# Block tables built in four parts, one branch at the end, output row numbers computed earlier

## The chip, the cores and the metric

The kernel runs on one core of one Trainium2 chip. The time is that of one whole launch, in device microseconds; of a kernel the median of several runs is given. Inputs and outputs lie in the chip's memory, and every step of the computation is in the launch.

## The reference

Three stages follow each other, in float32:

```
attention: state = alpha_t * state + k_t v_t^T ;  y_t = q_t state     (4 batches, 8 heads, 768 steps, 48 wide)
x = y as (3072 tokens, 384)
MoE 1, dense:  h = max(x @ w_in, 0);  x = (h * h) @ w_out              (384 -> 2048 -> 384)
MoE 2, top 1:  logits = x @ w_gate (8 experts);  e = argmax;  gate = softmax(logits)[e]
               eom = sigmoid(x @ w_output_gate)
               out[token] = gate * eom[e] * (max(x @ w1[e], 0) @ w2[e])  (384 -> 1024 -> 384)
```

Which expert a token goes to, and so how many tokens an expert has, is known only in the run.

## The kernel before

Tokens are handled in 24 tiles of 128, three tiles to a group (`GT`, 8 groups `NG`). Matrices that need float32's accuracy are split into two float16 halves (high and low) and multiplied in three passes; a row of a tile is scaled by a power of two that comes from its largest magnitude (`normalize`: `mxx`, `ebx`, `invx`, then the halves of `xr`, which DMA transposes to `xT`).

The first part of the program, up to about 551 us, is not written in its order. Each step (`add`) has a due time (`nominal(g, n)`: group g, n 28ths into it), an engine, a cost and the steps it depends on; `Plan.emit` simulates the engines and takes on each free engine the ready step with the smallest due time. Steps with two possible engines go to the second when the first is too far behind. A step is emitted whole: what it issues on an engine stands there in one piece. To this part belong the attention (`attend`), MoE 1 (`moe1_in`: h = x times w_in, `moe1_out`: o), the normalised rows of its result (`x2_out`: `row`), the routing of groups 0 to 6, and the splitting of w1 and w2 into halves (`split`: the load `spw`, the halves `spo`, a check `spj`, the store).

The second part is a loop written by hand over blocks of 128 tokens of one expert: b from 0 to 27 and one turn more to finish. A turn computes `s1(b, 0)` and `s1(b, 1)`, each eight 128-wide pieces' half of h: matmuls `hb`, then `part` (ScalarE copies, VectorE adds, twice per half), `rb` on ScalarE, and the two halves `hh` on VectorE. Beside it stand `s2(b - 1, ...)` (matmuls `ob`, ScalarE's `ot`, and a GpSimd DMA that writes 128 rows to their places in the output, by the row numbers `oi`), the gather of a later block's tokens by GpSimd (`gather`), and the transposes of the next block's tokens on TensorE (`turn_block`: `rt_ps`, copied by ScalarE to `xtb`).

Which tokens and which expert a block has stands in a table, computed by `table` in two pieces, from the counts of tokens per expert (a matmul, `pc`). The early table (groups 0 to 5 routed; 7 blocks, `NBA`) is one step of the planned part, `first_table`, due at `nominal(6, 14)`. The late table (the other 24 blocks) is a generator that the block loop advances: in the turn of block 2 its first part and its second part, in the turn of block 3 all that is left, before the gather of block 7. The loop stops at 28 blocks (`NBS`); if the counts need more (`more_i`), a first branch at the end runs blocks 28 to 30, and if a check of value ranges failed (`flag_i`), a second one runs a general version of everything. With these inputs neither is taken.

The functions that the change touches follow, with their line numbers.

Of the kernel before, what the change touches and what calls it, by code (L numbers as in the profile page):

```python
# [19 lines left out]
P = 128  # L20
NB, NH, NS, HD = 4, 8, 768, 48
NT = NB * NS
DM = 384
# [168 lines left out]
def moe_chain_kernel(ctx, tc, qka, vv, wi, wo, wg, w1, w2, out):  # L192
# [850 lines left out]
    def table(last):  # L1043
# [30 lines left out]
        lim = rt.tile([P, NE], F32, name="lim")  # L1074
        V.scalar_tensor_tensor(out=lim, in0=cnt, scalar=-1.0, in1=eoff, op0=ALU.add, op1=ALU.add)
        bb = rt.tile([P, NBB], F32, name="bb")[:, 0:nb]
        hi_ = rt.tile([P, 1], I32, name="hi_")
# [7 lines left out]
        if last:  # L1085
            V.tensor_scalar(out=more_i, in0=tot, scalar1=float(NBS - NBA), scalar2=None,
                            op0=ALU.is_gt)
        yield
        R = [P, nb, NE]
# [7 lines left out]
        if not last:  # L1097
# [14 lines left out]
            op=ALU.mult)  # L1112
        V.tensor_reduce(out=st, in_=big3, axis=AX.X, op=ALU.add)
        V.tensor_tensor(
            out=ohb, in0=ohb, in1=lim.rearrange("p (a e) -> p a e", a=1).to_broadcast(R),
# [108 lines left out]

    flag_i = const.tile([P, 1], I32, name="flag_i")

    def raise_flag():
# [43 lines left out]
    def raise_flag2(a):  # L1271
        V.tensor_reduce(out=a[:, 4:5], in_=rsum, axis=AX.X, op=ALU.max)
        V.scalar_tensor_tensor(out=a[:, 5:6], in0=a[:, 4:5], scalar=60000.0, in1=a[:, 0:1],
                               op0=ALU.is_le, op1=ALU.mult)
        pf = ps_r.tile([P, 1], F32, name="pf", tag="r")
        T.matmul(pf, onesf, a[:, 5:6], start=True, stop=True)
        V.tensor_scalar(out=flag_i, in0=pf, scalar1=float(P), scalar2=None, op0=ALU.is_lt)

# [37 lines left out]

    def load_w(b, k):
        if b >= lim[0]:
            return
        if k == 0:  # L1320
            wreg[b] = (nc.sync.value_load(e_i[0:1, b:b + 1], min_val=0, max_val=NE - 1),
                       nc.sync.value_load(ld_i[0:1, b:b + 1], min_val=0, max_val=1))
        e, ld = wreg[b]
        src = (w1s, w2s)[k]
        with tc.If(ld > 0):
            nc.sync.dma_start(
                out=wslot[b % NSLOT][k].rearrange(("p a c m -> p (a c) m",
                                                   "p a (c j) m -> p (a c) (j m)")[k],
                                                  **({}, {"j": 2})[k]),
                in_=src[bass.ds(e, 1)].rearrange(("e a c p m -> p (e a c) m",  # L1330
                                                  "e a c p j m -> p (e a c) (j m)")[k]))

    def s1(b, half):
# [4 lines left out]
        if half == 0:  # L1338
            c["hh"] = late[2].tile([P, 2, NFE, P], F16, name="hh", bufs=3)
        hh = c["hh"]  # L1340
        r = late[2].tile([P, 4, P], F32, name="rb")
# [22 lines left out]
    def s2(b, half):  # L1364
# [13 lines left out]
        if half == 1:  # L1378
            ot = late[2].tile([P, DM], F32, name="ot", bufs=2)
            row = c["row"]  # L1380
            S.activation(out=ot, in_=o, func=AF.Copy, scale=row[:, DM:DM + 1].bitcast(F32))  # L1381
            oi = late[2].tile([P, 1], I32, name="oi", bufs=3)
            V.tensor_tensor(out=oi, in0=row[:, DM + 1:], in1=pad_i[:, b:b + 1],
                            op=ALU.add)
            G.indirect_dma_start(  # L1385
# [4 lines left out]
    def switch_to_splits():  # L1390
        cvs.close()
        sp_pool[0] = sps.enter_context(tc.tile_pool(name="sp", bufs=2))

    def switch_to_blocks():
        sps.close()
        early.close()
        late[0] = lateS.enter_context(tc.tile_pool(name="late", bufs=2))
        for s in range(NSLOT):
            wslot[s] = (late[0].tile([P, 2, ND, EF], F16, name=f"w1_{s}", bufs=1),
                        late[0].tile([P, 2, NFE, DM], F16, name=f"w2_{s}", bufs=1))  # L1400

# [4 lines left out]
    def first_table():  # L1406
        r = ring("r_ps", 1)
        return add(nominal(NG - 2, 14), "V", 6643, lambda: list(table(False)), [route_done[NG - 3]],
                   new=[r])

    with tc.manual_schedule():
# [47 lines left out]
        for b in range(NBS + 1):  # L1459
# [11 lines left out]
            if b == 3:  # L1471
                for _ in tabling:
                    pass
                gather(b + 4)
            s1(b, 1)
            if b == 0:
                turn_last(1)
# [13 lines left out]
            s2(b - 1, 0)  # L1491
            if b == 2:
                tabling = table(True)
                next(tabling)
            if b >= 3:
                gather(b + 5)
# [6 lines left out]
            s2(b - 1, 1)  # L1503
            if b == 2:
                next(tabling)
            for n in loaded:
                exponent_check(n)
            if b >= 1:
                load_w(b - 1 + NSLOT, 1)
        more = nc.values_load(more_i[0:1, 0:1], min_val=0, max_val=1)  # L1510
        with tc.If(more > 0):
            lim[0] = NBLK
            for b in range(NBS, NBLK):
                load_w(b, 0)
                load_w(b, 1)
                gather(b)
                transp(b)
                for h in range(2):
                    s1(b, h)
                for h in range(2):  # L1520
                    s2(b, h)
            raise_flag2(fa)
        lateS.close()
# [174 lines left out]

    flag = nc.values_load(flag_i[0:1, 0:1], min_val=0, max_val=1)
    with tc.If(flag > 0):  # L1700
        fallback()

# [44 lines left out]
```

## Time and profile before

| | us |
|---|---|
| runs, median (lowest to highest) | 808.29 (807.83 to 808.43) |
| the profiled execution | 805.57 |
| its span in the profile | 803.8 |
| mean granted clock of TensorE | 0.969 of full speed |
| TensorE busy | 752.1 (94%) |
| VectorE busy | 588.5 (73%) |
| ScalarE busy | 506.5 (63%) |
| GpSimd busy | 347.1 (43%) |

TensorE is busy nearly throughout, so a microsecond is to be won where it waits or runs at its lower clock. The shares are means over stages with different limits; the sections below go by single stretches. PE is TensorE, DVE VectorE, ACT ScalarE, POOL GpSimd, SP SyncE (it issues most DMAs); a q behind the name is an engine's sequencer. L1048 is a line of the kernel.

### The profile page before, as it was taken

How to read it: one execution, taken by the hardware profiler on the slowest of the kernel's cores; microseconds unless marked ns; L12 is line 12 of the kernel's file. 1: busy time of each engine (PE TensorE's matmuls, PEld its weight loads, DVE VectorE, ACT ScalarE, POOL GpSimd, SP SyncE). 2: the span in 40 equal slices, each digit the busy share in tenths (PEclk: the TensorE clock that was granted, in tenths of full speed). 3: DMA queues.
4: the chain of work that ended last, by engine and by line, in shares of the span. 5: the costliest groups of instructions: out<-in, count | busy, mean ns of one | idle time of the engine just before them, and what ended most of it. 6: DMA issues, size and time to landing. Idle time of an engine off the chain costs nothing.

```text
span 803.8 us, 16848 instructions
## 1 busy us (share of the span) xinstructions
PE 752.1 (94%) x6066; PEld 514.9 (64%) x6066; DVE 588.5 (73%) x1370; ACT 506.5 (63%) x1167; POOL 347.1 (43%) x359
## 2 busy tenths in 40 slices
PE   8987789899997999999999997999989999999992
PEld 5755446665664666666666664657767777777871
DVE  7989969787887999999998886324745555555460
ACT  3378767676786888788887785644345555555540
POOL 4377736543464365586765551540132222232100
PEclk9999789999999999999999999999999999999996
DMA  9446661789949857969949747782739799892720
GB/s 265 112 134 173 180 184 50 207 236 295 313 125 280 239 145 197 275 169 239 259 121 300 191 120 227 190 311 83 263 96 348 250 355 356 272 387 94 246 74 21
DMA packets 156130, 168.48 MB, mean 210 GB/s; under 512 B 55340, under 2 KB 125004, under 8 KB 156032
## 3 DMA queue, kind: packets, MB, share of 16 engines
q1 hardware_dynamic: 150912, 152.25, 64.0%
q0 software_dynamic: 5120, 15.00, 5.6%
q8 instruction: 51, 0.84, 0.5%
q14 instruction: 47, 0.39, 0.1%
HBM read 120.52 MB, written 35.43 MB: 194 GB/s over the span
## 4 chain that ended last, share of the span: by engine, by line
PE 66%; DVE 15%; DMA 9%; issue 5%; ACT 2%; POOL 1%; SPq 0%; POOLq 0%; DVEq 0%; ACTq 0%
PE h L775 17%; PE o L814 15%; PE ob L1375 11%; PE hb L1352 8%; PE hb L1353 4%; DMA xT<-xr 3%; PE sp L597 2%; DMA x2T<-row 2%; DVE w L376 2%; PE idle L337 2%; DVE tb L370 2%; PE y L623 1%; DVE ta L364 1%; DMA a<-in_qka 1%; DMA spw<-in_w 1%
## 5 line engine op out<-in xcount | busy, mean ns | idle before, releaser
L775 PE MATMUL h<-xT,wi 128*128 128x384 f16 x1152 | 206.8, 333 | 24.3 <-DMA xT<-xr 14.8
L814 PE MATMUL o<-wo,g 128*128 128x385 f16 x1152 | 204.8, 331 | 2.3 <-POOL wo L391 1.4
L775 PEld LDWEIGHTS <-wi 128*128 128x128 f16 x1152 | 111.2, 99 | 102.2 <-issue 15.7
L312 POOL TENSOR_TENSOR g<-gg,g 128x384 f16<-128x384 f32 x115 | 125.3, 1098 | 90.0 <-ACT gg L793 58.8
L814 PEld LDWEIGHTS <-g 128*128 128x128 f16 x1152 | 111.0, 99 | 80.5 <-issue 7.2
L1352 PE MATMUL hb<-xtb,w 128*128 128x256 f16 x672 | 115.9, 275 | 3.8 <-ACT xtb L1306 3.7
L1375 PE MATMUL ob<-w,hh 128*128 128x384 f16 x672 | 117.8, 326 | 0.0
L1353 PE MATMUL hb<-xtb,w 128*128 128x128 f16 x672 | 114.1, 220 | 0.0
L1385 POOL DMA_INDIRECT out<-ot,oi x28 | 28.3, 1010 | 178.3 <-ACT ot L1381 127.3
L1375 PEld LDWEIGHTS <-hh 128*128 128x128 f16 x672 | 63.6, 98 | 37.0
L1161 DVE SCALAR_TENSOR_TENSOR spo<-spw,spo 128x768 f16<-128x768 f32 (+1 forms) x56 | 74.4, 1328 | 9.3 <-ACT spo L317 9.3
L1357 DVE TENSOR_TENSOR part<-hb,part 128x256 f32<-128x256 f32 x112 | 44.4, 420 | 48.4 <-ACT part L1356 43.7
L782 ACT ACTIVATE r<-h 128x384 f32<-128x384 f32 x107 | 51.4, 485 | 40.7 <-PE h L775 37.9
L1352 PEld LDWEIGHTS <-w 128*128 128x128 f16 x672 | 66.2, 99 | 9.8
L788 ACT ACTIVATE g<-r 128x384 f16<-128x384 f32 x128 | 66.1, 517 | 8.0 <-DVE r L784 6.4
L1353 PEld LDWEIGHTS <-w 128*128 128x128 f16 x672 | 66.3, 99 | 5.8 <-issue 4.2
L1358 ACT ACTIVATE rb<-part 128x512 f32<-128x512 f32 x56 | 35.3, 631 | 51.1 <-DVE part L1357 45.7
L793 ACT ACTIVATE gg<-r 128x384 f32<-128x384 f32 x126 | 64.6, 512 | 0.0
L1356 ACT ACTIVATE part<-hb 128x256 f32<-128x256 f32 x112 | 40.8, 380 | 32.7 <-PE hb L1353 29.1
L1167 ACT ACTIVATE spj<-spw 128x768 bf16<-128x768 f32 (+1 forms) x56 | 51.9, 927 | 7.9 <-DMA spw<-in_w 7.4
L1360 DVE CAST hh<-rb 128x512 f16<-128x512 f32 x56 | 24.0, 429 | 44.2 <-ACT rb L1358 30.8
L317 ACT ACTIVATE spo<-spw 128x768 f16<-128x768 f32 (+1 forms) x42 | 39.3, 935 | 22.1 <-DMA w1s<-spo 8.9
(275 smaller groups left out, 1276.2 us busy)
## 6 DMA issues: line engine op xcount, KB each, us to landing
w<-w1s SPq DMA_DIRECT2D x13, 1536.0 KB
w<-w2s SPq DMA_DIRECT2D x13, 1536.0 KB
a<-in_qka SPq DMA_DIRECT2D x63, 258.0 KB
spw<-in_w SPq DMA_DIRECT2D x24, 512.0 KB
w1s<-spo SPq DMA_DIRECT2D x24, 512.0 KB
spw<-in_w SPq DMA_DIRECT2D x32, 384.0 KB
w2s<-spo SPq DMA_DIRECT2D x32, 384.0 KB
raw<-in_wi SPq DMA_DIRECT2D x16, 384.0 KB
```

Source lines behind the costliest of these rows:

```text
L312: eng.tensor_tensor(out=out, in0=a, in1=b, op=ALU.subtract, saturate=True)
L775: T.matmul(c["h"], wi16[:, f, a, d], xT[g][:, ND * b + d], start=(n == 0), stop=(n == 8))
L782: S.activation(out=c["r"], in_=c["h"], func=AF.Relu, scale=2.0 ** -19)
L788: S.activation(out=g16[:, f, 0], in_=c["r"], func=AF.Square, saturate=True)
L793: S.activation(out=c["gg"], in_=c["r"], func=AF.Square)
L814: T.matmul(x2[i], g16[:, f, a, t * P:(t + 1) * P], wo16[:, f, b, 0:DM + 1], start=(f == 0 and n == 0), stop=(f == NFC - 1 and n == 2))
L1161: V.scalar_tensor_tensor(out=c["o"][:, 1, 0:N], in0=c["w"][:, 0:N], scalar=1024.0, in1=c["o"][:, 0, 0:N], op0=ALU.mult, op1=ALU.subtract, ...
L1167: S.activation(out=jk[:, 0:N], in_=c["w"][:, 0:N], func=AF.Square, accum_out=guard[:, C_SP + n:C_SP + n + 1])
L1352: T.matmul(h[:, j], w[:, 0, d, fs], both[:, d], start=(d == 0), stop=False)
L1353: T.matmul(h[:, j, 1], w[:, 1, d, fs], both[:, d, 0], start=False, stop=(d == ND - 1))
L1357: V.tensor_tensor(out=part[:, js], in0=h[:, :, 0], in1=part[:, js], op=ALU.add)
L1375: T.matmul(o, c["hh"][:, a, f], w[:, x, f], start=(f == 0 and n == 0), stop=(f == NFE - 1 and n == 2))
```

## The change

Four edits are made together.

1. The table's generator stops at other points, so that it has four parts: P1 to `lim`, P2 from `hi_` to `ohb`, P3 from `e_i` to the sum `st`, P4 the rest. The early table becomes four planned steps, due at `nominal(6, 22)`, each after the one before.
2. The late table's P1 stands behind `s2(2, 1)`'s second half in the loop's turn 2, hence early in turn 3; P2 comes before `s1(3, 1)`, P3 behind it, P4 before `s1(4, 1)`. The gathers of blocks 7 and 8 follow P4, one turn later than block 7's stood.
3. `any_i`, set if `more_i` or `flag_i` is, guards one outer branch, inside which both old branches lie.
4. `oi` is computed in `s1(b, 0)` instead of `s2(b, 1)`.

```
@@ table
         V.scalar_tensor_tensor(out=lim, in0=cnt, scalar=-1.0, in1=eoff, op0=ALU.add, op1=ALU.add)
+        yield
         bb = rt.tile([P, NBB], F32, name="bb")[:, 0:nb]
...
                             op0=ALU.is_gt)
-        yield
         R = [P, nb, NE]
...
         V.tensor_reduce(out=st, in_=big3, axis=AX.X, op=ALU.add)
+        yield
@@ raise_flag2
+        V.scalar_tensor_tensor(out=any_i, in0=pf, scalar=float(P), in1=more_i,
+                               op0=ALU.is_lt, op1=ALU.max)
         V.tensor_scalar(out=flag_i, in0=pf, scalar1=float(P), scalar2=None, op0=ALU.is_lt)
@@ s1
             c["hh"] = late[2].tile([P, 2, NFE, P], F16, name="hh", bufs=3)
+            c["oi"] = late[2].tile([P, 1], I32, name="oi", bufs=5)
+            V.tensor_tensor(out=c["oi"], in0=c["row"][:, DM + 1:], in1=pad_i[:, b:b + 1],
+                            op=ALU.add)
@@ s2
-            oi = late[2].tile([P, 1], I32, name="oi", bufs=3)
-            V.tensor_tensor(out=oi, in0=row[:, DM + 1:], in1=pad_i[:, b:b + 1],
-                            op=ALU.add)
+            oi = c["oi"]
@@ first_table
-        return add(nominal(NG - 2, 14), "V", 6643, lambda: list(table(False)), [route_done[NG - 3]],
-                   new=[r])
+        parts = table(False)
+        x = route_done[NG - 3]
+        for n in range(4):
+            x = add(nominal(NG - 2, 22), "V", 1700, lambda: next(parts, None), [x], new=[r] * (n == 0))
+        return x
@@ block loop
             if b == 3:
-                for _ in tabling:
-                    pass
+                next(tabling)
+            if b == 4:
+                next(tabling, None)
+                gather(b + 3)
                 gather(b + 4)
             s1(b, 1)
+            if b == 3:
+                next(tabling)
...
             s2(b - 1, 0)
-            if b == 2:
-                tabling = table(True)
-                next(tabling)
-            if b >= 3:
+            if b >= 4:
                 gather(b + 5)
...
             s2(b - 1, 1)
             if b == 2:
+                tabling = table(True)
                 next(tabling)
@@ end
-        more = nc.values_load(more_i[0:1, 0:1], min_val=0, max_val=1)
-        with tc.If(more > 0):
-            lim[0] = NBLK
...
-    flag = nc.values_load(flag_i[0:1, 0:1], min_val=0, max_val=1)
-    with tc.If(flag > 0):
-        fallback()
+    general = nc.values_load(any_i[0:1, 0:1], min_val=0, max_val=1)
+    with tc.If(general > 0):
+        more = nc.values_load(more_i[0:1, 0:1], min_val=0, max_val=1)
+        with tc.If(more > 0):
+            more_blocks()
+        flag = nc.values_load(flag_i[0:1, 0:1], min_val=0, max_val=1)
+        with tc.If(flag > 0):
+            fallback()
```

`more_blocks` is the old first branch's content with buffers of its own. Lines of the table below P1 are one higher in the new file, those of a block 12 to 14.

First place: VectorE around the early table, where a tile of the last group is normalised. Before, the table's last lines (`used`), then the tile's `mxx` to the low half of `xr`, with two low halves of weight pieces (`spo`) between:

```order
L1123 SCALAR_TENSOR_TENSOR st<-bidx,cin,st 128x7
L1125 TENSOR_SCALAR pad_i<-st 128x7
L1128 TENSOR_SCALAR used<-cbase 128x8
L1130 TENSOR_SCALAR used<-used 128x8
L1131 TENSOR_TENSOR used<-used,nblk 128x8
L416 TENSOR_REDUCE mxx<-y 128x1
L1161 SCALAR_TENSOR_TENSOR spo<-spw,spo 128x1024
L421 TENSOR_SCALAR ebx<-mxx 128x1
L1161 SCALAR_TENSOR_TENSOR spo<-spw,spo 128x1024
L427 SCALAR_TENSOR_TENSOR invx<-ebx,imax 128x1
L321 TENSOR_SCALAR xr<-y,invx 128x384
L437 SCALAR_TENSOR_TENSOR xr<-y,invx,xr 128x384
```

In the new order P1 ends (`lim`, L1075) directly ahead of `mxx`; then come one `spo`, `ebx`, and P2, whose last lines are the first three here:

```order
L1096 TENSOR_REDUCE eseq<-big_6772 128x7
L1098 TENSOR_SCALAR eseq<-eseq 128x7
L1100 TENSOR_TENSOR ohb<-eseq,eidx 128x56
L427 SCALAR_TENSOR_TENSOR invx<-ebx,imax 128x1
L1162 SCALAR_TENSOR_TENSOR spo<-spw,spo 128x1024
L437 SCALAR_TENSOR_TENSOR xr<-y,invx,xr 128x384
L1105 TENSOR_SCALAR e_i<-eseq 128x7
L1107 TENSOR_TENSOR st<-eseq 128x7
L1108 SCALAR_TENSOR_TENSOR ld_i<-bidx,cin,st 128x7
```

The low half of `xr` now stands ahead of P3 and P4 (P3 begins with `e_i`), and the high half (L321) is gone from VectorE: it is issued on ScalarE.

The counts of the early table come from TensorE's `pc`, which stood ahead of a tile's `y` and now stands between the halves of it. Before:

```order
L1046 LDWEIGHTS ones
L1046 MATMUL pc<-acc,ones 128x8
L623 MATMUL y<-ts,qf 128x96
L631 LDWEIGHTS ms
L631 MATMUL y<-vs,ms 128x48
```

and now:

```order
L631 MATMUL y<-vs,ms 128x48
L631 LDWEIGHTS ms
L631 MATMUL y<-vs,ms 128x48
L1046 LDWEIGHTS ones
L1046 MATMUL pc<-acc,ones 128x8
L623 MATMUL y<-ts,qf 128x96
```

Behind it, the matmuls of group 7 change places: 18 of h, then 12 of o, then 9 of h, where 9 of h and 12 of o took turns.

Second place: VectorE in the blocks' loop, around the late table. `part` x2 are the adds of one half of a block. Before, from the middle of P2 (`more_i`) over the first adds of block 3 to the start of P3:

```order
L1086 TENSOR_SCALAR more_i<-cin 128x1
L1383 ISA oi<-grow,pad_i 128x2
L1091 TENSOR_TENSOR big_8120<-bb,ctop 128x192
L1096 TENSOR_REDUCE eseq<-big_8120 128x24
L1100 TENSOR_TENSOR ohb<-eseq,eidx 128x192
L1357 TENSOR_TENSOR part<-hb,part 128x256 x2
L1325 UNCONDITIONAL_BRANCH
L1360 CAST hh<-rb 128x512
L1361 TENSOR_TENSOR hh<-rb,hh 128x512
L1105 TENSOR_SCALAR e_i<-eseq 128x24
L1107 TENSOR_TENSOR st<-eseq 128x24
L1108 SCALAR_TENSOR_TENSOR ld_i<-bidx,cin,st 128x24
```

Now, from the end of P1 over the first adds of block 3 (`oi` ahead of them is new here) and into P2, and then from P2's end over that block's second adds and P3 to the first adds of block 4:

```order
L1075 SCALAR_TENSOR_TENSOR lim<-cnts,eoff 128x8
L1352 ISA oi<-grow,pad_i 128x2
L1371 TENSOR_TENSOR part<-hb,part 128x256 x2
L1374 CAST hh<-rb 128x512
L1375 TENSOR_TENSOR hh<-rb,hh 128x512
L1341 UNCONDITIONAL_BRANCH
L1079 TENSOR_SCALAR hi__8155<-cin 128x1
```

```order
L1100 TENSOR_TENSOR ohb<-eseq,eidx 128x192
L1371 TENSOR_TENSOR part<-hb,part 128x256 x2
L1374 CAST hh<-rb 128x512
L1375 TENSOR_TENSOR hh<-rb,hh 128x512
L1341 UNCONDITIONAL_BRANCH
L1105 TENSOR_SCALAR e_i<-eseq 128x24
L1107 TENSOR_TENSOR st<-eseq 128x24
L1108 SCALAR_TENSOR_TENSOR ld_i<-bidx,cin,st 128x24
L1110 TENSOR_TENSOR big_8163<-ohb,start 128x192
L1113 TENSOR_REDUCE st<-big_8163 128x24
L1352 ISA oi<-grow,pad_i 128x2
L1371 TENSOR_TENSOR part<-hb,part 128x256 x2
```

Each part now stands between other adds; P4 (from L1115) follows one pair of adds further on.

Third place: GpSimd at the end of the program. Before, the untaken branches' contents lie between two pairs of a load and a branch:

```order
L1511 UNCONDITIONAL_BRANCH
L1511 ISA
L1511 UNCONDITIONAL_BRANCH
L1699 TENSOR_LOAD flag_i
L1700 COMPARE_AND_BRANCH
```

Now the outer branch comes first, and the old two lie inside it:

```order
L1722 TENSOR_LOAD any_i
L1723 COMPARE_AND_BRANCH
L1724 TENSOR_LOAD more_i
L1725 COMPARE_AND_BRANCH
L1292 DMA grow<-regions,idx_i 128x386
L1397 DMA out<-ot,oi 3072x384
```

The engine reads one value and branches once if nothing is to be done.

## Rows read from the trace of the kernel before

**Rows 1.** Waits of TensorE, 440 to 804 us (engine line waited for: us, times, longest)

```profile
PE h L775 <- DMA xT<-xr: 4.5, 1, 4.5
PE hb L1352 <- ACT xtb L1306: 3.7, 1, 3.7
```

**Rows 2.** Stretch: length, busy PE, PEld, DVE, ACT, POOL; granted clock, DMA share, GB/s

```profile
489.30:493.80 4.50, 0.07 (x1) 0.00 (x0) 2.22 (x8) 2.77 (x5) 0.00 (x0) 1.00 1.10 350
493.80:497.50 3.70, 3.67 (x13) 1.80 (x14) 1.60 (x7) 1.08 (x4) 0.00 (x0) 0.54 1.03 340
```

**Rows 3.** The chain that ended last: start us, us, what

```profile
487.28 6.42 DMA xT<-xr
```

**Rows 4.** Timeline of VectorE: start, us, operation, idle before and its releaser

```profile
474.93 0.17 DVE L1048 COPY cnt<-pc 128x8 f32<-128x8 f32 x1 [1.45 <-PE pc L1046]
...
478.76 0.17 DVE L1105 TENSOR_SCALAR e_i<-eseq 128x7 int32<-128x7 f32 x1
...
480.56 0.92 DVE L1122 TENSOR_TENSOR st<-st,lm 128x7 f32<-128x7 f32 x1
...
482.35 0.55 DVE L416 TENSOR_REDUCE mxx<-y 128x1 f32<-128x384 f32 x1
...
486.63 0.62 DVE L437 SCALAR_TENSOR_TENSOR xr<-y,invx,xr 128x384 f16<-128x384 f32 x1
```

**Rows 5.** Timelines of TensorE, GpSimd and ScalarE at the same place

```profile
475.43 0.31 PE L631 MATMUL y<-vs,ms 128*128 128x48 f16 x6
...
493.83 2.85 PE L775 MATMUL h<-xT,wi 128*128 128x384 f16 x9 [4.46 <-DMA xT<-xr]
...
480.55 0.91 POOL L312 TENSOR_TENSOR g<-gg,g 128x384 f16<-128x384 f32 x1 [3.80 <-ACT gg L793]
...
492.71 0.56 ACT L317 ACTIVATE row<-o,invz 128x384 f16<-128x384 f32 x1
```

**Rows 6.** Busy time by stretch, around a shorter wait of TensorE

```profile
86.60:91.00 4.40, 3.25 (x23) 2.09 (x21) 4.40 (x8) 4.14 (x11) 3.05 (x6) 1.00 0.62 153
```

**Rows 7.** Busy time by stretch: blocks 3, 4 and 5

```profile
573.90:585.93 12.03, 8.34 (x78) 6.35 (x78) 9.73 (x43) 4.04 (x11) 3.63 (x4) 1.00 0.58 187
585.93:595.94 10.01, 10.01 (x81) 7.59 (x80) 4.33 (x11) 4.10 (x10) 3.71 (x4) 0.83 0.28 79
595.94:604.13 8.19, 8.19 (x80) 6.37 (x79) 3.83 (x9) 4.26 (x10) 2.05 (x2) 1.00 0.56 152
```

**Rows 8.** Timeline of VectorE around the late table

```profile
575.75 0.15 DVE L1078 TENSOR_SCALAR hi__8084<-cin 128x1 int32<-128x1 f32 x1
...
577.92 0.75 DVE L1357 TENSOR_TENSOR part<-hb,part 128x256 f32<-128x256 f32 x2
...
580.53 0.17 DVE L1105 TENSOR_SCALAR e_i<-eseq 128x24 int32<-128x24 f32 x1
...
581.64 0.35 DVE L1114 TENSOR_TENSOR ohb<-ohb,lim 128x192 f32<-128x192 f32 x1
...
583.68 0.75 DVE L1357 TENSOR_TENSOR part<-hb,part 128x256 f32<-128x256 f32 x2
```

**Rows 9.** Timeline of VectorE in block 5, first and second adds

```profile
597.44 0.42 DVE L1357 TENSOR_TENSOR part<-hb,part 128x256 f32<-128x256 f32 x1 [2.27 <-ACT part L1356]
...
600.66 0.75 DVE L1357 TENSOR_TENSOR part<-hb,part 128x256 f32<-128x256 f32 x2
```

**Rows 10.** By line: operation xcount, duration ns min/median/max, first and last start us

```profile
L1511 POOLq COMPARE_BRANCH  x1: 57/57/57, 790.5 to 790.5; - x1
L1511 POOLq INC_SWDGE_SEM  x1: 1781/1781/1781, 790.9 to 790.9; - x1
...
L1700 PEldq COMPARE_BRANCH  x1: 5012/5012/5012, 790.3 to 790.3; - x1
L1700 POOLq COMPARE_BRANCH  x1: 45/45/45, 793.1 to 793.1; - x1
...
L1743 POOLq DRAIN  x3: 40/107/6611, 796.0 to 803.5; - x3
```

More of the change, by code (lines that the diff above doesn't have):

```diff
@@ L1225, in moe_chain_kernel @@
     flag_i = const.tile([P, 1], I32, name="flag_i")
+    any_i = const.tile([P, 1], I32, name="any_i")
     def raise_flag():
@@ L1315, in moe_chain_kernel, with load_w @@
     wreg = {}
-    def load_w(b, k):
+    def load_w(b, k, always=False):
         if b >= lim[0]:
@@ L1324, in load_w, with load @@
         src = (w1s, w2s)[k]
-        with tc.If(ld > 0):
+        def load():
             nc.sync.dma_start(
@@ L1331, in load_w @@
                                                   "e a c p j m -> p (e a c) (j m)")[k]))
+        if always:
+            load()
+        else:
+            with tc.If(ld > 0):
+                load()
     def s1(b, half):
@@ L1392, in switch_to_splits, with open_blocks @@
         sp_pool[0] = sps.enter_context(tc.tile_pool(name="sp", bufs=2))
+    def open_blocks(pools):
+        late[0] = pools.enter_context(tc.tile_pool(name="late", bufs=2))
+        for s in range(NSLOT):
+            wslot[s] = (late[0].tile([P, 2, ND, EF], F16, name=f"w1_{s}", bufs=1),
+                        late[0].tile([P, 2, NFE, DM], F16, name=f"w2_{s}", bufs=1))
     def switch_to_blocks():
@@ L1396, in switch_to_blocks @@
         early.close()
[L1397 to L1400, printed above, removed]
+        open_blocks(lateS)
     def zero_rows():
@@ L1509, in moe_chain_kernel @@
                 load_w(b - 1 + NSLOT, 1)
-        more = nc.values_load(more_i[0:1, 0:1], min_val=0, max_val=1)
-        with tc.If(more > 0):
-            lim[0] = NBLK
[L1513 to L1522, printed above, removed]
         lateS.close()
@@ L1697, in fallback, with more_blocks @@
                 SY.dma_start(out=out[bass.ds(ti * P, P), :], in_=res)
-    flag = nc.values_load(flag_i[0:1, 0:1], min_val=0, max_val=1)
-    with tc.If(flag > 0):
-        fallback()
+    def more_blocks():
+        lim[0] = NBLK
+        with tc.manual_schedule(), ExitStack() as pools:
+            open_blocks(pools)
+            late[2] = pools.enter_context(tc.tile_pool(name="blocks", bufs=2))
+            for b in range(NBS, NBLK):
+                load_w(b, 0, True)
+                load_w(b, 1, True)
+                gather(b)
+                transp(b)
+                for h in range(2):
+                    s1(b, h)
+                for h in range(2):
+                    s2(b, h)
+            raise_flag2(fa)
+    general = nc.values_load(any_i[0:1, 0:1], min_val=0, max_val=1)
[6 more added lines that the diff above has]
+            fallback()
 def _arrange(q, k, v, alpha, moe_w_in, moe_w_out, moe2_w_gate, moe2_w_output_gate, moe2_w1, moe2_w2):
```

## The prediction, made before the changed kernel ran

> **What bounds the kernel now.** I read the waits of TensorE first, then the stretches around the two long ones, then VectorE's instructions that they follow from, and the end of the program last. From 440 us to the end TensorE has two waits that count, 4.5 us for the transposed activations xT and 3.7 us for a block's transposed tokens xtb [rows 1]. So two places beside the tail are worth looking at, and both lie behind the block tables.
>
> The first is the early table. TensorE has almost nothing to do from 489.30 to 493.80, and its granted clock is 0.54 in the 3.70 us that follow, the lower of its two levels (1.2 GHz against 2.4) [rows 2]. Behind that no wait is listed until the blocks [rows 1]. The chain shows what was late: the transposes of group 7's last tile, 6.42 us from 487.28 [rows 3]. They start when VectorE has written the low half of that tile, xr, by 487.25 (486.63 + 0.62), and ahead of it the whole table ran in one piece, from cnt at 474.93 to the reduction mxx at 482.35, 7.42 us [rows 4]. The second is the late table: the block in which it is finished takes 12.03 us, the next 10.01 us at a mean clock of 0.83, the one after it 8.19 us [rows 7]. Together they are 3.84 + 1.82 = 5.66 us above two plain blocks.
>
> **Early table: 4.9 us (3.5 to 6.2).** The same instructions are issued; they stand elsewhere. Of the four parts, P1 and P2 stay ahead of xr, P3 and P4 (from e_i at 478.76 to mxx at 482.35, 3.59 us) now stand behind it. The high half of xr moves to ScalarE, where it stands early in the queue; that takes an instruction as long as the low half's 0.62 us off VectorE [rows 4]. Against this, TensorE's count pc now stands behind the first half of a tile's y: its last matmuls begin at 475.43 [rows 5], so cnt begins about 475.64 instead of 474.93, 0.71 later. One cast of a weight piece comes to VectorE ahead of cnt, where the engine waited 1.45 us for pc [rows 4]; I price it at nothing, and at up to 0.7 if it starts late. So xr is ready at 487.25 − 3.59 − 0.62 + 0.71 = 483.75. The transposes take their 6.42 us again and the 0.13 between their end and the matmul is kept (493.83 − 487.28 − 6.42 [rows 3, 5]), so h begins at 490.3, 3.5 us earlier; TensorE's older work ends 4.46 before its h, at 489.37 [rows 5], so a stall of about 0.9 is left. Such a stall does not bring the lower clock: from 86.60 to 91.00 TensorE was idle for 4.40 − 3.25 = 1.15 us and the clock stayed at 1.00 [rows 6]; it fell behind idle times of 4.5 and 3.7 [rows 1, 2, 7]. The half-clock stretch then goes too, 3.70 × (1 − 0.54) = 1.70 us [rows 2]. What is late next: in the new order 18 matmuls of h come first, then 12 of o, which need an accumulator that ScalarE's row frees. That row ran at 492.71 for 0.56 us [rows 5], held up by a load of weights and not by the table, so I leave it there; with the low half behind it the accumulator is free about 493.5, and the 18 matmuls (2 × 1.43 at full clock, half of the 2.85 that nine took at 0.54 [rows 5]) end about 493.2. That gives 0.3 back. Sum 3.5 + 1.7 − 0.3 = 4.9. TensorE has no other wait before the blocks [rows 1], so the lead reaches the first of them. Bounds: 6.2 if the stall vanishes whole (4.46 + 1.70), 3.5 if VectorE gets to xr 1.4 later than I say (4.9 − 1.4).
>
> One thing speaks against the new place. The compare st at 480.56 took 0.92 us, beside a GpSimd multiplication that ran from 480.55 for 0.91 [rows 4, 5], while neighbours of its size took 0.17 [rows 4]. P2 will now run at about that time, with several instructions of the same kind.
> The Trainium skill, "SBUF — State Buffer", section "SBUF: two separate sides", says that VectorE and GpSimd share a port pair as a lock: an instruction of VectorE with two inputs from that memory, beside one of GpSimd that reads it, waits for the whole of the other. The two rows agree with it; by that rule P2 would lose up to 0.75 us, and the sum would be 0.7 smaller. That is inside the bounds above.
>
> **Late table: 3.9 us (−2.2 to 5.7).** Before, P1, P2 stand ahead of one pair of adds (part) and P3, P4 ahead of the next. By the starts of its rows P2 is 577.92 − 575.75 = 2.17 us (with an oi in it), P3 1.11, P4 2.04 [rows 8]. Now P1 stands ahead of block 3's first adds, where VectorE is idle for over 2 us in a plain block [rows 9]; P2 ahead of its second adds; P3 behind them; P4 ahead of block 4's second adds. In the plain block from 595.94 the second adds start at +4.72 [rows 9]; from such adds to the next block's first matmul is 585.93 − 583.68 = 2.25 us [rows 7, 8]. So a plain block has 8.19 − 4.72 − 2.25 = 1.22 us of slack. P2 eats it and leaves 0.95 us of waiting, P4 leaves 0.82, P1 and P3 nothing: P3 falls before the next block's first adds at +1.50, where VectorE waits too. Both waits are shorter than the 1.15 us that left the clock alone [rows 6], so no half-clock stretch follows. Gain 5.66 − 1.77 = 3.9. If P2 and P4 are wholly exposed it is 5.66 − 4.21 = 1.4; if each also brings a half-clock stretch like the block of 10.01 us, 1.4 − 2 × 1.82 = −2.2; if all hide, 5.7. I take the value by the slack, since it is worked out from a block of the same make. The gathers of blocks 7 and 8 come a block later; each is used three or four blocks on, so I cost them at nothing; if one came late, the block would wait for its gather.
>
> **The end: 0.8 us (−1.3 to 2.6).** Before, each engine passes two branches. GpSimd reads the first at 790.5, spends 1.78 us on a semaphore of its queue from 790.9, reads the second at 793.1, and begins the final drain at 796.0: 2.9 us for that second jump [rows 10]. With one outer branch there is one jump and the same semaphore instruction behind it: 790.5 + 2.9 + 1.8 = 795.2 against 796.0. If the jump takes as long as TensorE's second (5.01 us [rows 10]) the end is 1.3 later; if the semaphore instruction runs beside the jump's fetch, 2.6 earlier. TensorE reads its second branch at 790.3 [rows 10]; it reads its only one no later than that, and with the same 5.0 us is through by 795.3, no longer than GpSimd. If the drain of 6.6 us ends at a fixed time, the gain is nothing.
> The Trainium skill, "Runtime: NRT & Kernel Launch", section "Instruction fetch mechanics", says that a taken branch to a place outside what is already fetched stalls until that is loaded. By that rule each jump stalls and one jump fewer is worth a whole 2.9 us on GpSimd. The trace agrees for the second jump and not for GpSimd's first, behind which it went on 0.4 us later.
>
> **Small edits.** any_i is one short instruction on VectorE, beside one of the same kind. oi is moved half a block, not added; ahead of the adds it takes at most what e_i takes, 0.17 us [rows 4], out of the 1.22 of slack, and VectorE is busy for 3.83 of 8.19 us there [rows 7]. I cost both at nothing; without that cover they would be 0.2 a block.
>
> **Sum.** 4.9 + 3.9 + 0.8 = 9.6 us from the profiled run's 805.57 (its span 803.8 and 1.8 around it), that is 796.0. The runs' median is 808.29, 2.7 above that run, so I forecast 808.29 − 9.6 = 798.7.
>
> **Rivals.**
> (a) The first lead is given back: ScalarE's queue and the weight loads are what the next matmuls wait for (the row at 492.71 hints at it [rows 5]; that TensorE had no gap later speaks against [rows 1]). Term one is then the half-clock stretch's 1.7 alone, and the time 808.29 − 6.4 = 801.9.
> (b) The late pieces are not hidden and the lower clock follows both: −2.2 for term two, 808.29 − 3.5 = 804.8. For it: the idle before block 4 was followed by 0.83. Against: each piece is near 2 us and the slack 1.22.
> (c) All waits vanish: 6.2 + 5.7 + 0.8 to 2.6, some 793.9 to 795.6. Against: 2.17 is above the slack.
> (d) Each jump costs what the second did: 4.9 + 3.9 + 2.9, 796.6. GpSimd's own first jump speaks against it.
> (e) Cutting the tables makes more waits that each pull the clock down. Four of them (before h, before o, in blocks 3 and 4) of 2.0 us each, each with its 1.7 us, are 14.8 against today's 4.46 + 1.70 + 5.66 = 11.8: 3.0 lost, and 0.8 won at the end, is 810.5, slower. It decides somewhere between an idle time of 1.15 us, which left the clock alone, and 3.7, which did not [rows 1, 6]; three of my four are at 0.9 or just above and one at 0.3.
> (f) The tables are not what the waits hang on, and another transfer takes their place at once: no change, about 808.
>
> **How the numbers follow.** Forecast 0.53 (its own range 796 to 801.5), (a) 0.15, (b) 0.11, (c) 0.06, (d) 0.05, (e) 0.05, (f) 0.05. Faster by over 0.2% (1.6 us, about what a measurement of this kernel can tell from no change) are the first five: 0.90; same 0.05; slower 0.05. The range 795.5 to 804.8 holds the forecast, (a), (d), and (b) up to its middle.
>
> **What would show it.** Right: no wait for xT over 1.2 us near 490, granted clock 1.00 behind it, the first block's matmuls about 5 us earlier, blocks 3 and 4 near 9 us each at clock 1.00, and GpSimd's final drain 0.8 us sooner relative to its branch. Wrong: a wait over 2 us near 493 with a low clock behind it; a block of 10 us or more among the first six; a time above 805.

## The result and the profile after

The changed kernel takes 799.56 us (median of 7 runs, 795.17 to 802.19) against 808.29 (7 runs, 803.32 to 811.59): ratio 0.9891, 95% interval 0.9860 to 0.9922, so 6.3 to 11.3 us less. Forecast were 798.7 us and a range of 795.5 to 804.8. Its profiled execution has a span of 800.5 us, 3.3 below that of the kernel before; that pair says less than the medians, for the changed kernel's profile came 3.5 us late to the place where the changes begin (the last 12 matmuls of o ahead of pc start at 476.23 instead of 472.72), and up to there both issue the same instructions in the same order on every engine. In the 14 profiles of this study that start lies between 470.6 and 477.8. So the readings below are lengths of stretches within one profile.

The waits of TensorE in the changed kernel, from 440 us on (engine, line, what was waited for: us, times, longest), which answer to [rows 1]:

```profile
PE hb L1366 <- ACT xtb L1310: 2.2, 3, 0.9
PE ob L1389 <- SPq L1341: 1.3, 2, 0.7
PE h L775 <- ACT r L782: 1.1, 1, 1.1
PE lg L912 <- DMA x2T<-row: 0.5, 1, 0.5
PE lg L912 <- issue: 0.5, 1, 0.5
PE rt_ps L1309 <- ACT x2T L1310: 0.3, 1, 0.3
```

The wait of 4.5 us for xT is gone, the 3.7 for xtb has become 2.2 in three pieces, and there are new small ones. VectorE's timeline in the changed kernel at the early table (start, us, operation), to set beside [rows 4]:

```profile
479.20 0.17 DVE L1048 COPY cnt<-pc 128x8 f32<-128x8 f32 x1 [1.62 <-PE pc L1046]
...
480.91 0.55 DVE L416 TENSOR_REDUCE mxx<-y 128x1 f32<-128x384 f32 x1
...
484.15 0.66 DVE L1098 TENSOR_SCALAR eseq<-eseq 128x7 f32<-128x7 f32 x1
...
486.18 0.61 DVE L437 SCALAR_TENSOR_TENSOR xr<-y,invx,xr 128x384 f16<-128x384 f32 x1
486.71 0.87 DVE L1105 TENSOR_SCALAR e_i<-eseq 128x7 int32<-128x7 f32 x1
```

and TensorE's there:

```profile
476.23 2.13 PE L814 MATMUL o<-wo,g 128*128 128x385 f16 x12
...
482.79 10.00 PE L814 MATMUL o<-wo,g 128*128 128x385 f16 x60
492.63 3.09 PE L775 MATMUL h<-xT,wi 128*128 128x384 f16 x18
```

Counted from the last 12 of o ahead of pc, cnt starts at +2.97 (before +2.21) and the low half of xr is written at +10.56 (before 487.25 − 472.72 = 14.53). h follows o with no idle time listed. By stretch (length, busy time of PE, PEld, DVE, ACT, POOL, granted clock, DMA share, GB/s), the 3.67 us from the start of h, and then blocks 3, 4 and 5, which answer to [rows 2] and [rows 7]:

```profile
492.63:496.30 3.67, 3.67 (x24) 2.24 (x23) 2.99 (x14) 3.21 (x7) 0.00 (x0) 1.00 0.95 290
...
573.81:583.10 9.29, 8.35 (x78) 6.37 (x78) 7.04 (x30) 4.03 (x11) 2.11 (x3) 1.00 0.67 200
583.10:592.35 9.25, 8.36 (x79) 6.35 (x79) 6.88 (x23) 4.04 (x11) 3.90 (x4) 1.00 0.25 84
592.35:600.54 8.19, 8.19 (x79) 6.35 (x78) 3.83 (x10) 3.98 (x10) 3.23 (x3) 1.00 0.55 154
```

The clock is 1.00 in all of them, and blocks 3 and 4 take 18.54 us. Before, they took 12.05 + 9.84 = 21.89 us from first matmul to first matmul (block 5 starts at 595.77; the second window of [rows 7] was 0.17 too long). At the end GpSimd has one branch (POOLq; rows by line, to set beside [rows 10]):

```profile
L1723 POOLq COMPARE_BRANCH  x1: 57/57/57, 787.9 to 787.9; - x1
L1723 POOLq EVENT_SEMAPHORE  x5: 17/17/43, 790.8 to 791.1; - x5
L1723 POOLq INC_SWDGE_SEM  x1: 1776/1776/1776, 791.2 to 791.2; - x1
...
L1771 POOLq DRAIN  x3: 40/107/6611, 793.0 to 800.2; - x3
```

The jump took 2.9 us (787.9 to 790.8), with five short semaphore instructions behind it until 791.2; the drain took the same 6.61. From the end of ScalarE's last ot (786.74 + 0.58) to the drain are 5.7 us, from the branch to the drain 5.1 (before 796.0 − 790.5 = 5.5).

### The profile page after: what moved, and what is told of

The parts are those of the page before. It is cut to its first block, busy times and chain, and to the rows that moved or that the text cites. A ratio compares the mean times of both kernels' runs of the same rounds, so it can differ in the third digit from the quotient of the medians.

```text
span 800.5 us, 16828 instructions
## 1 busy us (share of the span) xinstructions
PE 747.0 (93%) x6066; PEld 510.8 (64%) x6066; DVE 590.2 (74%) x1373; ACT 504.7 (63%) x1165; POOL 346.3 (43%) x359
## 5 line engine op out<-in xcount | busy, mean ns | idle before, releaser
L1366 PE MATMUL hb<-xtb,w 128*128 128x256 f16 x672 | 114.2, 273 | 2.2 <-ACT xtb L1310 2.2
L317 ACT ACTIVATE spo<-spw 128x768 f16<-128x768 f32 (+1 forms) x40 | 37.3, 934 | 19.3 <-DMA w2s<-spo 10.8
```

The costliest lines, as they stand in the source:

```text
L1366: T.matmul(h[:, j], w[:, 0, d, fs], both[:, d], start=(d == 0), stop=False)
```

## The experiments

For each kernel three stretches are read from its profile: "lead", from the last 12 of o ahead of pc to the first hb (before 78.51 us, changed 74.56); "loop", from there to the start of the last block (225.31 and 223.81); and "end", from the end of the last ot to the end of the span (14.50 and 13.15). Of times the ratio to the kernel before is given, with its interval, since each group of runs had its own runs of that kernel. The edits are shown shortened, with remarks in them that the kernels do not have.

**The four edits, one at a time.** The early table alone:

```
-        return add(nominal(NG - 2, 14), "V", 6643, lambda: list(table(False)), ...)
+        for n in range(4):
+            x = add(nominal(NG - 2, 22), "V", 1700, lambda: next(parts, None), [x], ...)
```

> Only the early table is built in four planned parts; the late table, the branches and oi stand as before. My theory: TensorE's wait for xT of group 7 (4.46 us before) and the 3.70 us at granted clock 0.54 behind it vanish, worth 6.2 us there, and about 2 us come back as new waits before the blocks, so that the stretch from the last 12 matmuls of o ahead of pc to the first hb shrinks by about 4.0 us (78.5 before) and the time by 0.4 to 0.6%. Rival A (nothing is given back without the other edits): 6.2 us, 0.7 to 0.8%. Rival B (the wait only moves): under 2 us, below 0.25%. Blocks 3 and 4 stay at 12.0 and 9.8 us under all three.

Ratio 0.9949 (0.9915 to 0.9983). The lead is 73.76 us, 4.75 less; blocks 3 and 4 stay at 12.00 and 9.85. No wait for xT is left in its list, but one for ScalarE's r is there, as in the changed kernel:

```profile
PE hb L1357 <- ACT xtb L1311: 3.8, 2, 3.6
PE h L775 <- ACT r L782: 1.3, 1, 1.3
PE rt_ps L1310 <- ACT x2T L1311: 0.2, 1, 0.2
PE lg L912 <- DMA x2T<-row: 0.2, 1, 0.2
```

So far that fits my theory; the last run below took away the part on what is given back. The late table alone:

```
             if b == 3:
-                for _ in tabling: pass      # P3 and P4 ahead of the second adds
+                next(tabling)               # P2; P3 behind s1(3, 1), P4 ahead of s1(4, 1)
```

> Only the late table is cut at the new places; the early table stays one step, branches and oi as before. My theory: blocks 3 and 4 take 9.2 to 9.3 us each at granted clock 1.00 instead of 12.05 and 9.84, 3.3 us less, and part of it is given back where TensorE's ob waits for weights in block 8 (0.7 us) because the loads of two experts' weights and the range checks' words fill the DMA queues there; the loop is 1.5 to 2.7 us shorter, the time 0.2 to 0.35% lower. Rival A (the give-back needs the lead of the early table too): no wait of ob, 3.3 us, 0.4%. Rival B (the gain of the blocks needs oi out of VectorE's way, which is not so here): blocks 3 and 4 at 9.5 or more, under 2.5 us.

Ratio 0.9965 (0.9928 to 1.0003). Loop 221.65 us, 3.66 less, with blocks of 9.30 and 9.07 and no wait of ob at all: rival A, as far as one run tells. The branch alone:

```
+    with tc.If(general > 0):
         with tc.If(more > 0): ...
         with tc.If(flag > 0): ...
```

> Only the two branches at the end are put inside one. My theory: GpSimd saves one jump of about 2.9 us but still makes one and the semaphore instruction behind it; from ScalarE's last ot to the final drain's start 6.7 us before, about 6.2 now, 0.4 to 0.8 us less, at most 0.1% of the time. Rival A (each jump costs 2.9 us): 2.9 us less, 0.35%. Rival B (the drain ends with the last output's landing): no change of the end.

Ratio 0.9974 (0.9943 to 1.0005). From the last ot's end at 792.66 to the drain at 798.6 are 5.9 us, 0.8 less than before, and the whole end is 13.33, 1.2 less. Neither rival fits: the end did not gain the 2.9 us of a jump, and the drain does start sooner. But from the branch to the drain are 5.3 us, only 0.2 less than before:

```profile
L1716 POOLq COMPARE_BRANCH  x1: 57/57/57, 793.3 to 793.3; - x1
...
L1764 POOLq DRAIN  x3: 40/107/6611, 798.6 to 805.7; - x3
```

The other 0.6 us is that the last output is issued 0.3 us behind ot instead of 0.9; why the branch alone does this is not shown. oi alone:

```
 def s1(b, half): if half == 0:
+            V.tensor_tensor(out=c["oi"], in0=c["row"][:, DM + 1:], in1=pad_i[:, b:b + 1], op=ALU.add)
```

> Only oi is computed earlier, in the first half of its own block. My theory: nothing in the blocks, and at the end the last output's DMA is issued 0.3 us behind ot instead of 0.9, because the output before it no longer waits for oi; 0.5 to 0.6 us, under 0.1%. Rival A (as predicted, nothing anywhere): the last output still comes 0.9 us behind ot. Rival B (oi pushes VectorE's adds in every block): 28 blocks longer than 8.20 us by 0.05 or more, 1.5 us or more slower.

Ratio 0.9993 (0.9957 to 1.0028). Plain blocks stay at 8.19 to 8.20, but for block 13 (8.50) and block 19 (8.39, before 8.34). The end is 13.88, 0.6 less, and the last output leaves 0.3 us behind ot, as my theory has it. The price shows in the first turns, which I had not said: 14.11, 8.74 and 12.21 us up to block 4 against 13.97, 8.68 and 12.05. The branch alone also brought the last output to 0.3 us behind ot, so the two gains at the end overlap: 1.2 + 0.6 alone, 1.35 together; and the reason that I gave, that the output before it no longer waits for oi, is not shown, since there oi stands where it stood. The intervals of the late table, the branch and oi reach 1.0000: these three are shown by the stretches of one profile each, not by the times.

**What of the early edit matters.** First the due time without the cut:

```
+        return add(nominal(NG - 2, 22), "V", 6643, lambda: list(table(False)), ...)
```

> The changed kernel, but the early table is one step again, with the later due time nominal(6, 22). It tells the due time from the cutting. My theory (what counts is how much of the table stands ahead of xr on VectorE): all four parts are still ahead of mxx, so xr is ready 0.7 us later than in the kernel before, TensorE has 12 matmuls of o more to do first (2 us) and then waits 3 to 3.5 us for xT, with a granted clock near 0.55 in the 3.5 us behind it; from the last o ahead of pc to the first hb some 78 us, 3.5 to 4.5 more than in the changed kernel. Rival (the due time does it): no wait over 1.2 us, within 1 us of the changed kernel there. Blocks 3 and 4 at 9.2 to 9.3 us under both.

Ratio 0.9912 (0.9875 to 0.9949), lead 76.89. The stretches of its trace from the end of o on:

```profile
488.20:491.30 3.10, 0.03 (x1) 0.00 (x1) 2.87 (x8) 1.82 (x5) 0.00 (x0) 1.00 0.98 347
491.30:495.00 3.70, 3.70 (x14) 1.85 (x15) 1.58 (x2) 2.04 (x4) 0.00 (x0) 0.61 1.12 328
```

The idle time of 3.1 us and the lower clock are as expected, though what TensorE waits for is 12 matmuls of o whose accumulator VectorE's row frees, not xT. The lead is 2.3 us above that of the changed kernel's first profile, where 3.5 to 4.5 were expected; that profile has 2.1 us of waits that come and go (below), and without them the changed kernel's lead is 72.5, so that the difference is 4.4. Then the cut without the due time:

```
+            x = add(nominal(NG - 2, 14), "V", 1700, lambda: next(parts, None), [x], ...)
```

> The changed kernel, but the four parts of the early table have the old due time nominal(6, 14). The planner then puts P1 to P4 all ahead of xr, with mxx and ebx between them. My theory: xr's low half is written only about 0.5 us earlier than in the kernel before, TensorE waits 3.4 to 4.2 us for xT at the lower clock afterwards, and the stretch from o to the first hb is 3.5 to 5 us longer than in the changed kernel. Rival (cutting alone does it, since the small normalising steps now run between the parts): a wait under 1.2 us and no lower clock, within 1 us of the changed kernel.

Ratio 0.9837 (0.9779 to 0.9895), lead 74.23: a miss. All four parts are ahead of xr, but xr is written at 486.73, 13.6 us behind the o at 473.16 (14.5 before), and TensorE waits 2.00 us, not 3.4 or more. And that idle time is not followed by the lower clock:

```profile
489.80:491.80 2.00, 0.01 (x1) 0.00 (x0) 1.16 (x2) 1.48 (x2) 0.00 (x0) 1.00 1.16 340
491.80:495.50 3.70, 3.69 (x23) 2.24 (x23) 2.46 (x9) 2.62 (x7) 0.00 (x0) 1.00 1.05 374
```

So the cut is enough to remove more than half of the wait and all of the clock's part; the lead without waits that come and go stays 1.7 to 2.1 us above the changed kernel's. But the earlier xr is the smaller share of it: h starts 2.46 us sooner behind the last 12 of o ahead of pc than before (18.65 for 21.11), 0.96 of it from xr, and 1.50 because from xr's end to h are 5.08 us instead of 6.58. Why the transposes were quicker is not shown.

**What the lower clock costs.** The kernel before, with work on TensorE in its wait:

```
+            if b == 3:
+                for n in range(16):
+                    T.matmul(fill, busy[:, 0:P], busy, start=True, stop=True)
```

> The kernel before, with 16 matmuls of zeros (512 columns, result unused, about 3.4 us) on TensorE while it waits for the transposed tokens of block 4. Nothing else is changed, the wait stays as long. My theory: block 3 still takes 12.05 us, and block 4, which follows without idle time, runs at granted clock 1.00 and takes 8.2 us instead of 9.84: 1.6 us less, 0.2%. Rival (the lower clock is not from the idle time but from something else in that stretch): block 4 stays at 9.8. A second rival: the extra work lengthens block 3, as it starts late and pushes the matmuls of block 4; then block 3 is 12.5 or more.

Blocks 3 and 4 in its trace:

```profile
578.44:590.45 12.01, 11.94 (x95) 7.94 (x94) 9.71 (x43) 4.04 (x11) 3.51 (x4) 1.00 0.59 194
590.45:598.64 8.19, 7.99 (x78) 6.27 (x77) 4.77 (x11) 4.19 (x11) 3.54 (x4) 1.00 0.33 96
```

The wait is as long as before, and block 4 takes 8.19 us at 1.00 instead of 9.84: 1.65 us for the clock alone, shown by taking nothing away but the idleness (time: 0.9966, 0.9932 to 0.9999).

**Where VectorE has room.** The late parts ahead of first adds:

```
+            if b in (2, 3, 4): next(tabling, None)      # P1, P2, P4, at a turn's end
+            if b == 4: next(tabling)                    # P3, ahead of s1(4, 1)
+            if b == 5: gather(7); gather(8); gather(9)
```

> The changed kernel, but the late table's P2 and P4 stand ahead of the first adds of blocks 4 and 5, P3 ahead of block 4's second adds, and the gathers of blocks 7 to 9 in the turn of block 5. By my theory of the slack (2.27 us of idle VectorE ahead of the first adds, 1.22 ahead of the second) nothing of P2 (2.2), P3 (1.1) and P4 (2.0) is seen by TensorE: blocks 3, 4 and 5 take 8.2 to 8.5 us, the loop is 1.7 to 2.0 us shorter than in the changed kernel, the time 0.2% lower. Rival A (the slack is shared by a whole block, not one place): blocks 4 and 5 at 8.8 or more. Rival B (the gathers come too late): a wait for the tokens of block 7 or 8 of over 1 us.

Ratio 0.9840 (0.9788 to 0.9892). Blocks 3 to 5:

```profile
574.27:582.46 8.19, 8.19 (x78) 6.37 (x78) 6.04 (x25) 4.10 (x10) 1.37 (x2) 1.00 0.74 231
582.46:590.82 8.36, 8.36 (x81) 6.38 (x79) 6.05 (x20) 4.15 (x10) 2.53 (x3) 1.00 0.19 71
590.82:599.01 8.19, 8.19 (x79) 6.37 (x79) 5.91 (x19) 4.18 (x10) 5.16 (x5) 1.00 0.46 133
```

No wait of TensorE is listed at the ends of these three blocks; blocks 3 and 4 are 2.0 us below the changed kernel's 18.54. VectorE's busy time in blocks 3 to 5 is 18.00 us, against 17.75 in the changed kernel, so the work is not less; but it is spread over three blocks here and over two there. That the place counts, and not the load of a block, shows between the second adds of block 3 and those of block 4. Here P2 and P3 stand there, 2.37 and 1.21 us by the starts of the rows:

```profile
581.76 0.15 DVE L1079 TENSOR_SCALAR hi__8249<-cin 128x1 int32<-128x1 f32 x1
...
584.13 0.15 DVE L1352 CUSTOM_DVE_ANT_0 oi<-grow,pad_i 128x2 uint16<-128x2 uint16 x1
...
587.36 0.33 DVE L1105 TENSOR_SCALAR e_i<-eseq 128x24 int32<-128x24 f32 x1
...
588.57 0.75 DVE L1371 TENSOR_TENSOR part<-hb,part 128x256 f32<-128x256 f32 x2
```

In the changed kernel it is P3 and P4, 1.21 and 1.94 us:

```profile
583.58 0.33 DVE L1105 TENSOR_SCALAR e_i<-eseq 128x24 int32<-128x24 f32 x1
...
584.79 0.15 DVE L1352 CUSTOM_DVE_ANT_0 oi<-grow,pad_i 128x2 uint16<-128x2 uint16 x1
...
588.16 0.35 DVE L1115 TENSOR_TENSOR ohb<-ohb,lim 128x192 f32<-128x192 f32 x1
...
590.10 0.75 DVE L1371 TENSOR_TENSOR part<-hb,part 128x256 f32<-128x256 f32 x2
```

3.6 us with the longer part ahead of the first adds cost TensorE no wait, 3.15 us with the longer part ahead of the second adds cost 0.89.

**Is what comes back due to the change?** The changed kernel had waits near 515 us (h for r) and in blocks 8 and 19 (ob, put down to SP's queue, where two experts' weights and the words of the range checks are loaded). Three variants and the changed kernel again, on one chip:

```
-CK0 = 5
+CK0 = 9        # first turn that loads the checks' words
```

> The four early parts with the old due time and the late table's parts ahead of first adds, as in the two runs before, and the loads of the range checks' words begin in the turn of block 9 instead of 5. My theory: TensorE's wait of ob for weights in block 8 (0.3 to 0.8 us in the kernels with a new early table) comes from those loads, which share the DMA queues with two experts' weights there; block 8 takes 8.20, the loop some 220.2 us, from the last o ahead of pc to the first hb 74.2; in all 11.5 to 13 us below the kernel before, 1.4 to 1.6%. Rival (the loads are not the cause): block 8 at 8.5 to 9.0 as in the others.

> The same without the later checks: the four early parts with the old due time, the late parts ahead of first adds. Loop 220.6 to 221.2 us with 0.3 to 0.8 us of waiting of ob in block 8, from o to the first hb 74.2; 11 to 12.5 us below the kernel before, 1.35 to 1.55%. If the two edits were not to add up (rival), one of the two stretches is back at its length in the changed kernel, 223.8 or more for the loop.

> The changed kernel with the checks' loads from the turn of block 9 on. My theory: block 8 takes 8.20 instead of 9.03 us, and in block 19, where two experts' weights come again beside the checks, the wait stays (up to 0.8 us); loop 222.9 to 223.3 us. Rival: block 8 stays at 8.4 to 9.0.

> The changed kernel again, beside the others on one chip. By theory the stretch from o to the first hb is 74 to 75 us with 1 to 2 us of waits for ScalarE's r or the transposes x2T near 500 to 520, blocks 3 and 4 are at 9.2 to 9.3, block 8 is 0.2 to 0.9 us over 8.20. If the waits near 515 and in block 8 are chance of one run (rival), they are absent here, and the stretch is below 73 us, block 8 at 8.20.

| | ratio (interval) | lead | loop | block 8 | block 19 |
|---|---|---|---|---|---|
| early due 14, late ahead of first adds, checks from 9 | 0.9878 (0.9839 to 0.9917) | 74.17 | 221.70 | 8.19 | 9.95 |
| the same, checks from 5 | 0.9857 (0.9821 to 0.9892) | 74.02 | 221.59 | 9.47 | 8.43 |
| changed kernel, checks from 9 | 0.9848 (0.9820 to 0.9876) | 72.21 | 222.77 | 8.20 | 8.97 |
| changed kernel again | 0.9812 (0.9763 to 0.9860) | 72.56 | 222.15 | 8.20 | 8.19 |

The list of waits of the changed kernel's second profile, from 440 us on:

```profile
PE hb L1366 <- ACT xtb L1310: 2.1, 3, 0.9
PE lg L912 <- DMA x2T<-row: 0.4, 1, 0.4
PE rt_ps L1309 <- ACT x2T L1310: 0.3, 1, 0.3
```

The same program, without the wait for r and without those for ob: whether such a wait comes, and how long it is, is chance of one execution, and my theory of a give-back of fixed size falls. It does not fall whole. Over the five profiles with the early table in four parts at the later due time, the lead is 74.56, 73.76, 74.00, 72.21 and 72.56, with 2.1, 1.4, 1.7, 0 and 0.4 us of waits for r and the logits' transposes in it, 1.1 in the mean; taking them off leaves 72.2 to 72.5 in each. In the nine other profiles no such wait is listed in that stretch. So the new order makes them likelier, as far as 14 profiles tell. Waits of ob in block 8 are listed in four of the six profiles with both new tables and the checks from turn 5, and in no other; in block 19 they are also in kernels with the old tables (1.8 us with the branch alone, 0.4 with the filled wait). Whether the checks make such waits likelier stays open: the two runs with the later checks had none in block 8, but neither had the second changed kernel. No variant is shown to beat the changed kernel in time: its two comparisons with the kernel before gave 0.9891 and 0.9812, and that is 6 us apart, more than the 2.0 us of the late parts.

## Why the prediction was right

**Early table, forecast 4.9 us, bounds 3.5 to 6.2.** In the five profiles with the old early table the lead is 78.2 to 79.7 us, 78.8 in the mean, and in the five with four parts at the later due time 73.4 in the mean: 5.3 us, and 6.5 without the waits that come and go. The step that was mis-sized is "The transposes take their 6.42 us again". In the three profiles of the new order that tell of the landing they took 3.4 us; the changed kernel's second profile has

```profile
L751 SPq DMA_TRANSPOSE xT<-xr x1: 1419/1419/1419, 483.8 to 483.8; - x1
...
DMA to landing us min/median/max: 3.4/3.4/3.4
```

There h starts at 489.65, 16.40 us behind the last 12 of o ahead of pc, as in the first profile, so xT lay ready for 2.4 us, and the "stall of about 0.9" is gone: TensorE is busy up to h. Why the transposes are shorter is open. SyncE issued four loads and stores of weights in the 2.6 us ahead of them before and one store now, but no run varies that. xr came 4.0 us earlier instead of 3.5. The later cnt was right (0.76 for 0.71); the difference is mainly that an `spo` took 1.87 us beside a GpSimd multiplication before (482.81) and takes 1.21 now (481.38), less what P2 lost (next). The 0.3 for o's accumulator did not show behind these 18 of h. The pricing of the half-clock stretch at 1.7 us is borne out by the filled wait (1.65), at another place. That 4.9 came near the mean is in part luck: the stall of 0.9 and the 0.3 that fell away stand against 1.1 us of waits that came back, which the forecast priced at nothing.

**The shared port.** In the changed kernel an instruction of P2 (L1098, 0.66 us, before 0.17) ends at 484.81, beside a GpSimd multiplication of 483.87 to 484.78, and e_i (0.87) ends at 487.58 beside one of 486.64 to 487.55:

```profile
483.87 0.91 POOL L312 TENSOR_TENSOR g<-gg,g 128x384 f16<-128x384 f32 x1 [3.49 <-ACT gg L793]
486.64 0.91 POOL L312 TENSOR_TENSOR g<-gg,g 128x384 f16<-128x384 f32 x1 [1.86 <-ACT gg L793]
```

P2 lost 0.5 us, within the 0.75 that I weighed; e_i belongs to P3, which stands behind xr. Both instructions that were held have one tensor input, where the prediction spoke of two. The Trainium skill ("SBUF — State Buffer", "SBUF: two separate sides") has the pair held for the whole instruction, and names, beside instructions of VectorE with two inputs, those in a 2-port mode. The trace agrees with the whole instruction (both end 0.03 us behind the multiplication); whether these two ran in such a mode no run here shows.

**Late table, forecast 3.9 us.** Blocks 3 and 4 gained 21.89 − 18.54 = 3.35 us. The two waits are 0.94 and 0.89 us for the 0.95 and 0.82 worked out from the slack, with the clock at 1.00; the difference is that TensorE is busy for 8.35 and 8.36 us in these blocks and not 8.19, and the 0.17 of the window. That the slack is one place's, not a block's, is shown by the parts ahead of first adds.

**The end, forecast 0.8 us.** It gave 1.35, and only the smaller part by the forecast mechanism. From the branch to the drain are 5.1 us (5.3 with the branch alone) for 5.5 before: 0.2 to 0.4, not 0.8. The step that failed is the sum "790.5 + 2.9 + 1.8": it leaves out the 0.4 us between a jump and the semaphore instruction of the queue, which stood behind the old first branch too (790.5 to 790.9 [rows 10]). The rest was priced at nothing: the last output leaves 0.6 us sooner behind ot, which oi alone and the branch alone each bring about, and from the drain's start to the end of the span are 7.4 us instead of 7.8. So it is luck that with the branch alone the drain came 0.8 sooner behind ot. "I cost both at nothing" failed for oi also in the first turns, where it cost about 0.3. Rival (d), a jump of 2.9 us saved whole, is refuted: the whole end gained less. The jump over the long body took 2.9 us in the changed kernel as before; behind the old first branch GpSimd went on 0.4 us later [rows 10]. The Trainium skill ("Runtime: NRT & Kernel Launch", "Instruction fetch mechanics") has a taken branch stall where its target is not yet fetched. The trace agrees with a stall at one of these two jumps; what had been fetched it does not show.

**Sum.** 6.5 (the lead without the waits that come and go) + 3.35 − 0.4 (blocks 0 to 2, part of it from oi) + 1.35 = 10.8 us; with those waits it is 5.3 for the lead and 9.6 in all. The two measured differences of medians are 8.7 and 14.8. The forecast of 9.6 was right in sign and size, and in the mechanism of the two tables; at the end the mechanism was right only in part. The second set's median, 793.99, lies 1.5 us below the range, and no stretch accounts for that, so whether a set of runs falls into the range is in part chance. Of the rivals, (a) happened in part in some executions; of (c) the early wait vanished whole and the late ones did not; (b), (e) and (f) did not happen.

## What to carry to other kernels

A long helper step that a planner issues whole costs its full length to whatever stands behind it in an engine's queue; cut it, and put the pieces where that engine is seen to wait, for the slack is that of a place and not of a block. A wait of TensorE of 3 us or more is to be priced with the slow stretch behind it, as nearly all such waits here had one. And one profile's new waits have no price until the same kernel has been profiled again.

## What was not expected of the hardware

An idle time of 2.0 us was followed by a granted clock of 1.00 in the run with parts due at 14, while around one of 2.0 us in the kernel before the mean was 0.74 (187.30 to 193.40 us):

```profile
187.30:193.40 6.10, 4.13 (x26) 2.72 (x26) 4.96 (x12) 4.12 (x8) 1.26 (x1) 0.74 1.11 352
```

So the length of the idle time alone does not decide. Counted in the 14 traces between 60 and 760 us, where the granted clock was full ahead of the idle time: of 34 idle times of 1.0 to 1.5 us none was followed by a mean clock below 0.9 in the next 4 us, of 75 of 1.5 to 3 us 24 were, and of 38 longer ones 37. The one exception is in the run with parts due at 14:

```profile
253.41:256.90 3.49, 0.00 (x0) 0.00 (x1) 3.46 (x9) 2.30 (x6) 1.02 (x2) 1.00 1.15 331
256.90:260.60 3.70, 3.70 (x33) 2.36 (x34) 3.05 (x6) 2.03 (x5) 0.54 (x2) 1.00 0.98 332
```

For rival (e) the prediction put the limit between 1.15 and 3.7 us; the trace of the kernel before has idle times of 1.98, 2.00 and 2.22 us with the lower clock behind them (before 80.2, 189.3 and 152.4 us).

Programs with the same instructions up to the last 12 of o ahead of pc reached that place up to 7 us apart in 14 profiles. The changed kernel's two sets of runs have medians of 799.56 and 793.99, 0.7% apart, with 808.29 and 808.83 for the kernel before beside them, and the intervals here are 0.3 to 0.6% to each side. So the 0.2% that the prediction thought could be told apart is too little.
